# Block-end silu on other engines and a section later, transposes of the identity at the start, later stores of the split output weights

## The chip, the core and the metric

The kernel runs on one core of a Trainium2 chip. The metric is the device time of one execution in microseconds. The core's engines are TensorE (PE in the profile, its weight loads PEld), VectorE (DVE), ScalarE (ACT), GpSimd (POOL) and SyncE (SP), which here issues every DMA. Each engine works through its own queue in order; semaphores tie the queues together.

## The reference

One sequence of 2048 tokens with 576 features. The input is normalised and goes through two branches, whose product is added to the input:

```python
x = A_x
xn = _layernorm(x)
s = mha(xn, A_wqkv, A_wo)                    # 32 heads of 18, softmax, output projection
g = silu((gelu(xn @ B_w_gate) * (xn @ B_w_up)) @ B_w_down)   # 576 -> 4608 -> 576, tanh gelu
return x + s * g
```

All inputs and the output are float32.

## The kernel before

**Precision.** Matmul operands are kept as two parts, a rounded `hi` and the remainder `lo`, and most products are summed as hi·hi + lo·hi + hi·lo. `split` makes the parts on GpSimd (one `tensor_scalar`, one `tensor_tensor`), `split_av` on ScalarE and VectorE.

**Blocks.** Tokens are cut into NB = 4 blocks of TB = 512, four tiles of 128 each (index `j`).

**Prologue (pools `pro` and `pps`).** For block 0, `load_x` and `norm` bring in and normalise four tiles `xx`. `transposes` (line 205) turns them on TensorE against the identity `ident`: 20 transposes into five PSUM tiles `pt`, four tiles `j` by five slices `k`, all slices of one `j` first. `split_t` then writes the transposed activations `xth`, `xtl`, `xtr` from PSUM, ScalarE first and VectorE behind it. `project` (line 252) computes one 128-row tile of queries and keys per call, nine per block in the order `ORDER`, with 14 matmuls of 128x512 into a PSUM tile `po`; ScalarE and VectorE evict it and SP stores both parts to `qk` in DRAM. `values_of` does the values and stores them in `vs`. In the last block, `split_wo(n)` follows the projections 0 to 4: it loads a fifth of the output weights, splits it on GpSimd into two tiles `wo` (tag `rawp`, five buffers, shared with earlier weights) and stores both to `wos` in DRAM, from where they are read much later. These stores follow the load and the split directly in the program.

TensorE's order is written out by hand (`manual_schedule`); the order on the other engines is a scheduler's, except where `keep_in_program_order` holds an instruction. The DMAs, too, leave SP's queue in this order, and an issue that waits holds up all issues behind it.

**Main part.** The feed-forward branch is the spine. `section` (line 398) computes one 128-wide slice of the gate and up products for one token block: 27 pairs of matmuls into PSUM tiles `pg` and `pu`. There are 36 sections per block and 144 in all. Attention work (`specials`) is spread between the pairs: score maxima (`max_mm`, PSUM tile `pm` with three buffers, reduced on VectorE into `mx`), and scores for the exponentials (`score_mm`, PSUM tile `pe`, exponential on ScalarE into `pT`). At the end of a section `activate` applies the tanh GELU with ScalarE and VectorE; after it come the values' matmuls (`values`, PSUM `acc`), the down projection (`downs`, `down`, line 381, PSUM `py`) and `finish`, where GpSimd splits the activated slice into `hh` and `hl` and, every second section, the down weights into `dh` and `dl`. GpSimd also splits the next section's gate and up weights (`wh`, `wl`), and runs ahead of TensorE with them as far as the buffers let it.

**Down projection and block end.** A round of two sections gives one down projection, in two halves of two token tiles each, one section apart. Each half makes four pieces of 128x288 and adds them on VectorE into `Y`, the block's sum (line 387). `Y` is allocated anew in the first section of a block, in one buffer. In the last round of blocks 0 to 2 the half is followed by the silu of its four pieces, by `gate` (line 356): ScalarE computes `th = tanh(y/2)`, VectorE `(th + 1) * y` in place (line 359), and SP stores each 128x576 tile to `ys`. The factor one half comes later. The last block's pieces go through `gate` in the epilogue.

**Output projection.** `tasks` places its steps in later sections: `load_wo` reads `wos`, `load_xy` brings a piece of `x` and of `ys` into tiles `xx` (one buffer) and `yy` (two), `project_o` multiplies and adds, `store_y` writes `out`.

**The loop that matters to the change** (line 725): for each of its 128 passes `section`, the K, V and q loads, `tasks`, `values`, `downs`, `tasks`, `finish`. A block's last round ends in `downs` of the first two sections of the next block; in the span these are the sections that begin at 770.65 and 787.99, 1414.97 and 1432.32, 2059.83 and 2077.18 us.

Of the kernel before, what the change touches and what calls it, by code (L numbers as in the profile page):

```python
# [8 lines left out]
F32 = mybir.dt.float32  # L9
# [8 lines left out]
P = 128  # L18
# [33 lines left out]
def f(ap):  # L52
    return ap.bitcast(F32)
# [13 lines left out]
def kernel(ctx: ExitStack, tc: tile.TileContext, x, wqkv, wo, w_gate, w_up, w_down, out):  # L67
# [22 lines left out]
    def split(hi, lo, raw):  # L90
        first = nc.gpsimd.tensor_scalar(hi, raw, 1.0, 1.0, op0=ALU.mult, op1=ALU.mult)  # L91
        nc.gpsimd.tensor_tensor(lo, raw, f(hi), op=ALU.subtract)  # L92
        return first
# [41 lines left out]
    with tc.tile_pool(name="pro", bufs=1) as pro, tc.tile_pool(name="pps", bufs=1, space=PSUM) as pps:  # L135
# [45 lines left out]
        def norm(xr, b, between=None):  # L181
# [20 lines left out]
                nc.scalar.activation(xr[j][:, D:D + HR], xr[j][:, R0:D], AF.Copy)  # L202
            return last

        def transposes(b, xr):
            xt = XT[b % 2]
            pts = [pps.tile([P, TB], F32, name="pt", bufs=KT + 1) for k in range(KT + 1)]
            for j in range(4):
                for k in range(KT + 1):
                    nc.tensor.transpose(pts[k][:, j * P:(j + 1) * P], xr[j][:, k * P:(k + 1) * P], ident)  # L210
            for k in range(KT + 1):
                split_t(pts[k], k, xt)
            return xt
# [9 lines left out]
        VN = [pro.tile([P, H // 2, DH + 1], F32, name=f"vn{i}") for i in range(8)]  # L223
        for v in VN:
            nc.vector.memset(v, 1.0)
        ORDER = (4, 5, 0, 1, 6, 7, 8, 2, 3)
        WQK, WV = {}, {}

# [23 lines left out]
        def project(b, t, xt):  # L252
            o = pps.tile([P, TB], F32, name="po", bufs=3)
            mm_terms(o, WQK[t], slice(0, P), xt, all_t)
            hi, lo = tmp2("t1"), tmp2("t2")
            nc.scalar.activation(hi, o, AF.Copy)
            nc.vector.tensor_tensor(lo, o, f(hi), op=ALU.subtract)
            for i, a in enumerate((hi, lo)):
                nc.sync.dma_start(qk[i, t * P:(t + 1) * P, b * TB:(b + 1) * TB], f(a))
# [9 lines left out]
        def split_wo(k):  # L269
            n = min(KO, D - k * KO)  # L270
            raw = raw_tile([KO, D])
            tc.keep_in_program_order(nc.sync.dma_start(raw[0:n], wo[k * KO:k * KO + n, :]))
            hi, lo = (pro.tile([KO, D], F32R, name=f"wo{i}", tag="rawp", bufs=5) for i in range(2))
            split(hi[0:n], lo[0:n], raw[0:n])
            for i, t in enumerate((hi, lo)):
                nc.sync.dma_start(wos[i, k * KO:k * KO + n, :], f(t)[0:n])

        NQT = 2 * D // P
        def after(what, before):
# [19 lines left out]
        for b in range(NB):  # L299
            for n, t in enumerate(ORDER):  # L300
                if n == (2 if b == 0 else 0) and b + 1 < NB:
                    xr = load_x(b + 1)
                if b == 0 and ahead_qk:
                    first = split_qk(*ahead_qk.pop(0))
                    if n < 3:
                        after(first, last)
                    if n + 4 < NQT:
                        ahead_qk.append(load_qk(ORDER[n + 4]))
                if b == 0 and n == 4:
                    raw_r, VR = load_rest(2 * D, D)  # L310
                    split_av(VR[0], VR[1], raw_r, tc.keep_in_program_order)
                if b == 0 and n in (5, 6):
                    raw_v.append(load_wv(n - 5))
                if b == 0 and n in (7, 8):
                    split_wv(n - 7, raw_v[n - 7])
                project(b, t, xt)
                if b == NB - 1 and n < NK:
                    split_wo(n)
                if n == 4 and b + 1 < NB:
                    norm(xr, b + 1)  # L320
            store_xt(b, xt)
            nxt = transposes(b + 1, xr) if b + 1 < NB else None
            if b == 1:
                XD = load_xd(0)
            if b == 2:
                ahead = load_gu(0, tc.keep_in_program_order)
                for k in range(NG):
                    split_gu(ahead, k)
            for j in range(4):
                for c in range(2):  # L330
                    values_of(b, j, c, xt)
            xt = nxt
# [2 lines left out]
    ps = ctx.enter_context(tc.tile_pool(name="ps", bufs=1, space=PSUM))  # L335


    FF = {"w": ahead, "xd": XD, "down": [], "n": 0}
    finals = []

    def gate_up(tag):
# [14 lines left out]
    def gate(o, th, yy):  # L356

        nc.scalar.activation(th, yy, AF.Tanh, scale=0.5)
        nc.vector.scalar_tensor_tensor(o, th, 1.0, yy, op0=ALU.add, op1=ALU.mult)  # L359
# [11 lines left out]
    def down(b, r, hs, wd, Y, js):  # L371
        for j in js:
            tt = slice(j * P, (j + 1) * P)
            for c in range(2):
                cc = slice(288 * c, 288 * c + 288)
                py = ps.tile([P, 288], F32, name="py", tag="s", bufs=2)
                n = 0
                for g in range(G):
                    hh, hl = hs[g]
                    for a, w in ((hh, wd[0]), (hh, wd[1]), (hl, wd[0])):  # L380
                        nc.tensor.matmul(py, a[:, tt], w[:, g, cc], start=(n == 0), stop=(n == 3 * G - 1))  # L381
                        n += 1
                yy = Y[:, j, cc]
                if r == 0:
                    nc.vector.tensor_copy(yy, py)
                else:
                    nc.vector.tensor_tensor(yy, py, yy, op=ALU.add)  # L387
                if b == NB - 1 and r == NR - 1:
                    finals.append((Y, j, c))
        if b < NB - 1 and r == NR - 1:  # L390
            for j in js:
                t = b * 4 + j
                for c in range(2):
                    yy = Y[:, j, 288 * c:288 * c + 288]
                    gate(yy, ffn.tile([P, 288], F32, name="th"), yy)
                nc.sync.dma_start(ys[t * P:(t + 1) * P, :], Y[:, j, :])

    def section(specials=(), tag="f", raw_d=None, early=None):

        n = FF["n"]  # L400
        FF["n"] += 1
        b, r = divmod(n // G, NR)
        g = n % G
        pairs, pg, pu = gate_up(tag)
        if g == 0:
            FF["hs"] = []
            if r == 0:
                FF["Y"] = ffn.tile([P, TB // P, D], F32, name="Y")
        keep = tc.keep_in_program_order if n == NU * NA + len(FIRST) + 1 else lambda i: i
        nxt = load_gu((n + 1) % (NR * G), keep) if n + 1 < NF else None  # L410
        if nxt:
            for k in range(NG - 1):
                split_gu(nxt, k)
        if g == G - 1:
            raw = FF["rawd"] = raw_d() if raw_d else raw_tile([P, G, D])
            nc.sync.dma_start(raw, w_down[r * G * P:(r + 1) * G * P, :].rearrange("(g p) n -> p g n", p=P))
            if early:
                FF["wd"] = early(raw)
        for p in spread(pairs, specials):
            p()  # L420
        if nxt:
            split_gu(nxt, NG - 1)
        FF["w"] = nxt
        if n + 1 < NF and (n + 1) % (NR * G) == 0:
            FF["xd"] = load_xd(b + 1)
        FF["act"] = activate(pg, pu)
# [103 lines left out]
    def tasks(n, part):  # L530
        for t in todo.pop((n, part), []):
            t()
# [26 lines left out]
    with tc.tile_pool(name="att", bufs=1, reuse_waits="tile") as att:  # L559
# [32 lines left out]
        def load_q(u):  # L592
            j, g = divmod(u, NQ)
            cols = slice(j * TB, (j + 1) * TB)
            for r in range(2):
                t = QS[u, r] = att.tile([P, TB], F32R, name=f"q{r}", bufs=3)
                for a in range(2):
                    q = f(t)[64 * a:64 * a + MROW, :]
                    h = QD * g + 2 * r + a
                    rows = slice(h * DH, (h + 1) * DH)  # L600
                    for n, i in enumerate((0, 0, 1)):
                        nc.sync.dma_start(q[n * DH:(n + 1) * DH, :], qk[i, rows, cols])
# [122 lines left out]
        for n in range(NU * NA):  # L725
            u, i = divmod(n, NA)
            s0 = n * SLOTS
            section([p for s in range(s0, s0 + SLOTS) for p in slot_pairs(s)])
            if n > 0:
                load_k(n - 1 + KB)  # L730
            load_v(n + 2)
            if i == 1 and u + 2 < NU:
                load_q(u + 2)
            tasks(n, 0)
            um, im = divmod(s0 + LEAD + SLOTS, NS)
            if im == 0 and um <= NU:
                max_neg(um - 1)
            for kt in range(i * SLOTS // 2, (i + 1) * SLOTS // 2):
                values(u, kt)
            if im == 0 and um <= NU:  # L740
                max_end(um - 1)
            tasks(n, 1)
            downs()
            tasks(n, 2)
            finish()
# [86 lines left out]
```

## Time and profile before

| | us |
|---|---|
| median of 3 runs | 2670.77 |
| lowest and highest run | 2667.56, 2672.83 |
| the profiled execution | 2674.07 |
| its span, first to last instruction | 2672.3 |
| prologue, to the first `pg` matmul | 199.79 |
| a regular section, mean of four | 17.42 |

The profile is one execution, taken by the hardware profiler. A row of the timeline shows the start, the duration, the engine, the line and the operation with the tiles that it writes and reads; in square brackets, the idle time of the engine before it and what ended that. A row of the waits shows who waited for whom, the total, how often, and the longest. A row of the windows gives the stretch, its length, and each engine's busy time and number of instructions in it. A row of the groups has the smallest, median and largest duration in ns.

### The profile page before, as it was taken

The numbers are of one execution on the slowest core, as the hardware profiler recorded it, in microseconds if no ns is written. First come the engines' busy times: TensorE is split into PE (matmuls) and PEld (weight loads), VectorE is DVE, ScalarE is ACT, GpSimd is POOL, SyncE is SP. The second block draws the span as 40 slices with busy tenths as digits, with TensorE's granted clock in tenths as the row PEclk, the third lists the DMA queues.
The fourth block names the chain that finished last, engine by engine and source line by source line (L and its number), as shares of the span: only waits on it lengthen the run. The fifth ranks groups of instructions, "written<-read, shape, count | busy, mean of one in ns | idle before, by whom it ended". The sixth has DMA issues, their size and how long they took to land.

```text
span 2672.3 us, 55506 instructions
## 1 busy us (share of the span) xinstructions
PE 2648.8 (99%) x21000; PEld 2025.0 (76%) x21000; DVE 2007.3 (75%) x3432; ACT 1440.9 (54%) x2553; POOL 1354.0 (51%) x1439
## 2 busy tenths in 40 slices
PE   8999999999999999999999999999999999999999
PEld 7887777777777777777777777777777777777777
DVE  5327888888888877788888877788888877888445
ACT  3222466555666555566556655555666554666532
POOL 2117544544465555544456555554445556444563
PEclk9999999999999999999999999999999999999999
DMA  8866433344354334543346335433345454433341
GB/s 254 264 229 155 114 96 96 94 103 105 103 141 122 97 103 117 142 105 102 98 106 161 100 99 141 123 103 99 100 106 119 126 140 126 115 101 92 77 111 56
DMA packets 389143, 323.64 MB, mean 121 GB/s; under 512 B 105544, under 2 KB 302664, under 8 KB 388876
## 3 DMA queue, kind: packets, MB, share of 16 engines
q1 hardware_dynamic: 388876, 320.08, 44.8%
q8 instruction: 167, 2.74, 0.4%
q14 instruction: 100, 0.82, 0.1%
HBM read 266.58 MB, written 52.85 MB: 120 GB/s over the span
## 4 chain that ended last, share of the span: by engine, by line
PE 96%; DVE 2%; DMA 0%; ACT 0%; issue 0%; POOL 0%; SPq 0%; DVEq 0%
PE pg L351 27%; PE acc L673 17%; PE py L381 17%; PE pe L639 10%; PE pm L612 9%; PE pu L351 7%; PE po L156 7%; PE po L511 2%; DVE mx L613 1%; PE pt L210 0%; DVE Y L387 0%; DVE t L365 0%; DVE Y L359 0%; PE pm L622 0%; DMA xx<-in_A_x_dram 0%
## 5 line engine op out<-in xcount | busy, mean ns | idle before, releaser
L640 ACT ACTIVATE pT<-pe 128x512 f32<-128x512 f32 x2048 | 1165.3, 600 | 767.4 <-PE pm L612 610.7
L613 DVE TENSOR_REDUCE mx<-pm 128x1 f32<-128x512 f32 x2048 | 1295.2, 686 | 49.8 <-PE pm L612 29.2
L351 PE MATMUL pg<-xd,wh 64*128 64x512 f32 x2592 | 948.6, 398 | 0.5 <-issue 0.5
L351 PE MATMUL pu<-xd,wh 64*128 64x512 f32 x2592 | 946.5, 397 | 0.0
L639 PE MATMUL pe<-q,KS 56*128 56x512 f32 x2048 | 818.1, 407 | 0.1
L612 PE MATMUL pm<-KS,q 54*128 54x512 f32 x2048 | 799.5, 394 | 3.5 <-DVE mx L613 1.9
L91 POOL TENSOR_SCALAR wh<-raw 128x384 fp32r<-128x384 f32 x432 | 222.2, 515 | 882.6 <-DMA raw<-in_B_w_up_dram 516.0
L351 PEld LDWEIGHTS pg<-xd,wh 64*128 64x128 f32 x2592 | 483.3, 187 | 58.0 <-issue 22.6
L351 PE MATMUL pg<-xd,wl 64*128 64x512 f32 x1296 | 507.6, 392 | 0.0
L351 PE MATMUL pu<-xd,wl 64*128 64x512 f32 x1296 | 507.1, 391 | 0.0
L351 PEld LDWEIGHTS pu<-xd,wh 64*128 64x128 f32 x2592 | 483.6, 187 | 9.3 <-DVE t L368 1.4
L673 PE MATMUL acc<-pT,VS 128*32 128x512 f32 x4096 | 466.0, 595 | 0.0
L92 POOL TENSOR_TENSOR wl<-raw,wh 128x384 fp32r<-128x384 f32 x432 | 437.8, 1014 | 34.5
L639 PEld LDWEIGHTS pe<-q,KS 56*128 56x128 f32 x2048 | 369.3, 184 | 82.8 <-ACT pT L640 23.4
L612 PEld LDWEIGHTS pm<-KS,q 54*128 54x128 f32 x2048 | 377.2, 184 | 38.0 <-DVE mx L613 6.4
L387 DVE TENSOR_TENSOR Y<-py,Y 128x288 f32<-128x288 f32 x544 | 248.2, 457 | 203.5 <-PE py L381 202.6
L381 PE MATMUL py<-dh,hh 128*128 128x288 f32 x1152 | 357.6, 310 | 2.3 <-DVE Y L387 1.3
L381 PE MATMUL py<-dl,hh 128*128 128x288 f32 x1152 | 339.8, 295 | 0.0
L381 PE MATMUL py<-dh,hl 128*128 128x288 f32 x1152 | 338.5, 294 | 0.0
L673 PEld LDWEIGHTS acc<-pT,VS 128*32 128x32 f32 x4096 | 120.4, 109 | 275.8 <-issue 264.5
L381 PEld LDWEIGHTS py<-dh,hh 128*128 128x128 f32 x1152 | 216.0, 187 | 81.1 <-issue 41.1
L351 PEld LDWEIGHTS pg<-xd,wl 64*128 64x128 f32 x1296 | 242.1, 187 | 20.0
(110 smaller groups left out, 2811.6 us busy)
## 6 DMA issues: line engine op xcount, KB each, us to landing
KS<-qk SPq DMA_DIRECT2D x1536, 36.0 KB
raw<-in_B_w_gate_dram SPq DMA_DIRECT2D x144, 288.0 KB
raw<-in_B_w_up_dram SPq DMA_DIRECT2D x144, 288.0 KB
raw<-in_B_w_down_dram SPq DMA_DIRECT2D x68, 576.0 KB
VS<-vs SPq DMA_DIRECT2D x128, 152.0 KB
qk<-t SPq DMA_DIRECT2D x72, 256.0 KB
q<-qk SPq DMA_DIRECT2D x384, 36.0 KB
xd<-xhs SPq DMA_DIRECT2D x24, 384.0 KB
```

Of the source, the lines that this page charges most:

```text
L91: first = nc.gpsimd.tensor_scalar(hi, raw, 1.0, 1.0, op0=ALU.mult, op1=ALU.mult)
L92: nc.gpsimd.tensor_tensor(lo, raw, f(hi), op=ALU.subtract)
L156: nc.tensor.matmul(o, st, m, start=(i == 0), stop=(i == len(TERMS) - 1))
L351: nc.tensor.matmul(o, w[1 + wp][k][rr, c, :], xd[xp][k][rr, c, :], start=(i == 0), stop=(i == len(terms) - 1))
L381: nc.tensor.matmul(py, a[:, tt], w[:, g, cc], start=(n == 0), stop=(n == 3 * G - 1))
L387: nc.vector.tensor_tensor(yy, py, yy, op=ALU.add)
L511: nc.tensor.matmul(po[:, 0:288], o[x][0:n, k, :], OW[w][0:n, k, :], start=(m == 0), stop=(m == len(terms) - 1))
L612: nc.tensor.matmul(pm, QS[u, r][rr, t * P:(t + 1) * P], KS[(u * NA + c) % KB][r][rr, :], start=True, stop=True)
L613: nc.vector.tensor_reduce(MX[u][:, 2 * r + a, t, c:c + 1], pm, axis=AX.X, op=ALU.max)
L639: nc.tensor.matmul(pe, KS[(u * NA + c) % KB][r][rr, t * P:(t + 1) * P], QS[u, r][rr, :], start=True, stop=True)
L640: nc.scalar.activation(PT[u, kt][:, 2 * r + a, :], pe, AF.Exp, scale=SCALE)
L673: nc.tensor.matmul(ACC[u][32 * a:32 * a + 32, :], VS[(u * NA + c) % VB][:, v:v + 32], pt[:, a, :], start=(kt == 0), stop=(kt == NT - 1), s ...
```

## The change

- **Silu at block ends.** `down` no longer applies `gate` in blocks 0 to 2. It notes its pieces in a list, and a new function `gates`, called in every pass of the main loop between the loads and `tasks`, works on what is noted: ScalarE computes the tanh into a tile `th`, GpSimd adds one and multiplies by `Y` in two operations, and SP stores each 128x288 piece to `ys`. So each half is handled one section later than before. Three of the four tiles `th` take the buffers of `yy` and `xx`, which are not in use then.
- **One `Y`.** `Y` is allocated once, ahead of all blocks.
- **Identity transposes.** `warm(64)` issues 64 transposes of `ident` by itself into an unread `po` tile, ahead of the first transposes of block 0.
- **Stores of `wos`.** `split_wo` returns its tiles; `store_wo` stores them after the projection two later, held in program order.

```diff
+        def warm(n):
+
+            o = pps.tile([P, TB], F32, name="po", bufs=3)
+            for i in range(n):
+                nc.tensor.transpose(o[:, 0:P], ident, ident)
+
         def transposes(b, xr):
...
             for j in range(4):
+                if b == 0 and j == 0:
+                    warm(64)
                 for k in range(KT + 1):
...
             split(hi[0:n], lo[0:n], raw[0:n])
+            return k, n, hi, lo
+
+        def store_wo(k, n, hi, lo):
             for i, t in enumerate((hi, lo)):
-                nc.sync.dma_start(wos[i, k * KO:k * KO + n, :], f(t)[0:n])
+                tc.keep_in_program_order(nc.sync.dma_start(wos[i, k * KO:k * KO + n, :], f(t)[0:n]))
...
                 project(b, t, xt)
+                if b == NB - 1 and 2 <= n < NK + 2:
+                    store_wo(*parts.pop(0))
                 if b == NB - 1 and n < NK:
-                    split_wo(n)
+                    parts.append(split_wo(n))
...
-    FF = {"w": ahead, "xd": XD, "down": [], "n": 0}
+    FF = {"w": ahead, "xd": XD, "down": [], "gates": [], "n": 0,
+          "Y": ffn.tile([P, TB // P, D], F32, name="Y")}
...
         if b < NB - 1 and r == NR - 1:
-            for j in js:
-                t = b * 4 + j
-                for c in range(2):
-                    yy = Y[:, j, 288 * c:288 * c + 288]
-                    gate(yy, ffn.tile([P, 288], F32, name="th"), yy)
-                nc.sync.dma_start(ys[t * P:(t + 1) * P, :], Y[:, j, :])
+            FF["gates"] += [(b, j, c, Y) for j in js for c in range(2)]
+
+    def gates():
+
+        for k, (b, j, c, Y) in enumerate(FF["gates"]):
+            rows, cc = slice(b * TB + j * P, b * TB + (j + 1) * P), slice(288 * c, 288 * c + 288)
+            if k < 3:
+                th = op.tile([P, 288], F32, name="th", tag=("yy", "yy", "xx")[k], bufs=(2, 2, 1)[k])
+            else:
+                th = ffn.tile([P, 288], F32, name="th")
+            tc.keep_in_program_order(nc.scalar.activation(th, Y[:, j, cc], AF.Tanh, scale=0.5))
+            nc.gpsimd.tensor_scalar(th, th, 1.0, 1.0, op0=ALU.add, op1=ALU.mult)
+            nc.gpsimd.tensor_tensor(th, th, Y[:, j, cc], op=ALU.mult)
+            nc.sync.dma_start(ys[rows, cc], th)
+        FF["gates"] = []
...
         if g == 0:
             FF["hs"] = []
-            if r == 0:
-                FF["Y"] = ffn.tile([P, TB // P, D], F32, name="Y")
...
             load_v(n + 2)
             if i == 1 and u + 2 < NU:
                 load_q(u + 2)
+            gates()
             tasks(n, 0)
```

More of the change, by code (lines that the diff above doesn't have):

```diff
@@ L225 @@
             nc.vector.memset(v, 1.0)
+        parts = []
         ORDER = (4, 5, 0, 1, 6, 7, 8, 2, 3)
```

## The prediction

> **What bounds the kernel now.** I read the busy times first, then what TensorE (PE) waited for, then the length of like stretches, and last the timeline where these are longer than they should be.
>
> ```profile
> PE 2648.8 (99%) x21000; PEld 2025.0 (76%) x21000; DVE 2007.3 (75%) x3432; ACT 1440.9 (54%) x2553; POOL 1354.0 (51%) x1439
> ```
>
> PE is busy for 2648.8 of the 2672.3 us of the span; no other engine is above 76%. Time can be won where PE stands still, or where it keeps running with its matmuls further apart. The waits of PE alone list the first kind:
>
> ```profile
> PE pt L210 <- DVE xx L200: 10.9, 1, 10.9
> PE pm L612 <- DVE mx L613: 1.9, 4, 1.1
> PE pm L612 <- DMA q<-qk: 1.7, 2, 1.3
> ```
>
> The columns are total, number and longest. The start (10.9 us) and two later waits are all that matters. The second kind shows only in lengths. I cut the span at the first `pg` matmul of a section, so that each stretch below holds whole sections: four regular ones, then twice the four that follow a change of token block, then three with no block end and the three at the third block end.
>
> ```profile
> core 0 of [0], span 2672.3 us
> core 0: us, PE busy (x) PEld busy (x) DVE busy (x) ACT busy (x) POOL busy (x), PEclk, DMA share, GB/s
> 700.98:770.65 69.67, 69.67 (x572) 51.62 (x571) 57.09 (x96) 41.66 (x73) 37.16 (x39) 1.00 0.53 126
> 770.65:842.01 71.36, 71.11 (x571) 52.96 (x570) 60.66 (x104) 44.91 (x81) 40.02 (x42) 1.00 0.49 131
> 1414.97:1486.89 71.92, 71.57 (x572) 52.53 (x572) 61.16 (x104) 44.73 (x81) 41.18 (x43) 1.00 0.48 129
> 1990.15:2042.26 52.11, 52.11 (x427) 38.82 (x427) 42.27 (x70) 31.43 (x55) 29.73 (x31) 1.00 0.45 118
> 2059.83:2114.08 54.25, 53.96 (x428) 39.92 (x427) 46.21 (x78) 34.31 (x63) 37.68 (x36) 1.00 0.53 146
> ```
>
> The same PE work (571 or 572 matmuls; 427 or 428) takes 71.36 - 69.67 = 1.69, 71.92 - 69.67 = 2.25 and 54.25 - 52.11 = 2.14 us longer at the three block ends: 6.1 us. VectorE (DVE) and ScalarE (ACT) have eight instructions more there: the eight silu pieces.
>
> **Part 1, the silu.** The second half at one block end, in the timeline, and the group rows of its two operations:
>
> ```profile
> 1451.96 0.96 DVE L359 SCALAR_TENSOR_TENSOR Y<-th,Y 128x288 f32<-128x288 f32 x1
> 1452.84 0.68 DVE L613 TENSOR_REDUCE mx<-pm 128x1 f32<-128x512 f32 x1
> 1453.58 0.50 PE L612 MATMUL pm<-KS,q 54*128 54x512 f32 x1 [0.26 <-DVE mx L613]
> 1449.07 0.45 ACT L358 ACTIVATE th<-Y 128x288 f32<-128x288 f32 x1 [2.81 <-DVE Y L387]
> L358 ACT ACTIVATE th<-Y x24: 445/447/448, 786.2 to 2097.7; 128x288 f32<-128x288 f32 x24
> L359 DVE SCALAR_TENSOR_TENSOR Y<-th,Y x24: 448/696/1292, 786.9 to 2098.2; 128x288 f32<-128x288 f32 x24
> ```
>
> DVE takes its queue in order, and the silu products stand ahead of the reductions that free the score maxima's three PSUM buffers. The reduction of 1452.84 starts only behind the product of 1451.96, and PE waits for it at 1453.58. The change takes all 24 products off DVE (24 x 0.696 = 16.7 us of it); the additions into `Y` stay, and regular sections have those too. So I expect the excess of 6.1 us to go, and take 6.0. Upper bound 6.1.
>
> What it costs elsewhere. On ACT the four tanh of a half move from between the additions to the end of the next section, behind its GELU, where ACT stood idle 2.81 us (row of 1449.07). Four at 0.447 are 1.8 us and fit: nothing. Without that cover they would stand ahead of the exponentials, 1.8 us six times. On GpSimd (POOL) two operations per piece are new. Where they go, and who wants the work behind them:
>
> ```profile
> 802.17 0.51 POOL L91 TENSOR_SCALAR wh<-raw 128x384 fp32r<-128x384 f32 x1
> 802.76 1.02 POOL L92 TENSOR_TENSOR wl<-raw,wh 128x384 fp32r<-128x384 f32 x1
> 805.58 0.62 POOL L91 TENSOR_SCALAR hh<-t 128x512 fp32r<-128x512 f32 x1 [1.80 <-PE py L381]
> ...
> 809.06 2.75 POOL L92 TENSOR_TENSOR dl<-raw,dh 128x1152 fp32r<-128x1152 f32 x1
> 821.05 0.40 PE L381 MATMUL py<-dh,hh 128*128 128x288 f32 x1
> 824.46 0.49 PE L351 MATMUL pg<-xd,wh 64*128 64x512 f32 x1
> ```
>
> By elements a piece costs 0.51 x 288/384 + 1.02 x 288/384 = 1.15 us, a half 4.6 us (an estimate from these rows). The instruction order of the changed kernel puts the first half between `wl` (ends 803.78) and `hh` (805.58): 1.8 us of it fill an idle gap, and `hh`, `hl`, `dh` and `dl` come 2.8 us later. `dl` then ends at 814.6; PE asks for it at 821.05. The weight slices of 802.17 and behind are for the section that starts at 824.46, some 20 us on. The second half stands ahead of an `hh` that is wanted a section later still. So nothing again, with 6.4 us of slack. The stores of `ys` become 24 of half the size. They wait for GpSimd in SP's queue, ahead of two K loads, a V load, q loads and the next gate, up and down weights; the SP queue waited for the old stores at the same place, and these weights have those 20 us. Lower bound for this part: half of it, 3.0, should the added queueing of GpSimd reach the reductions in a way I don't see.
>
> **Part 2, the stores of the split output weights.** They stood in SP's queue right behind their load, so that SP waited for GpSimd's split, and later stores and loads with it:
>
> ```profile
> SPq L276 <- POOL wo L91: 8.4, 4, 4.1
> 187.97 0.41 ACT L266 ACTIVATE vn<-po 128x288 f32<-128x288 f32 x1 [1.01 <-PE po L156]
> 193.25 0.66 SPq L110 DMA_DIRECT2D raw<-in_B_w_gate_dram  x1
> 199.72 4.69 DMA vs<-vn
> 200.57 6.23 SPq L580 DMA_DIRECT2D KS<-qk  x12
> 206.85 3.95 SPq L602 DMA_DIRECT2D q<-qk  x11
> 209.35 0.46 PE L612 MATMUL pm<-KS,q 54*128 54x512 f32 x1 [1.34 <-DMA q<-qk]
> ```
>
> The first gate weights are issued at 193.25, though the value tile ahead of them was ready at 188.4: 4.9 us late. Their transfers are then still under way when the K loads begin: the last value store takes 4.69 us to land, and 12 K loads take 6.23 us where 11 q loads take 3.95 (0.36 each; 12 would take 4.3). The 1.9 us between are SP waiting for earlier transfers, and the q loads behind are what PE waits for (1.7 us in two waits). With the stores two projections later the split is done when their turn comes, the queue is level by 188, and the weights go up to 4.9 us earlier. Were all 1.9 us to go, the 1.7 us would go; were the memory itself the limit, nothing. The longest wait for a reduction (1.1 us, second row of PE's waits) comes ten microseconds later, and its chain leads back to that same landing by way of GpSimd's clearing of tiles. Bounds 0 and 1.7 + 1.1 = 2.8; I take 1.5, nearer the two q waits. The ten stores themselves cost nothing: the last is issued earlier than now.
>
> **Part 3, the idle transposes.**
>
> ```profile
> 1.01 0.29 POOL masks.py:199 TENSOR_SCALAR_AFFINE_SELECT ident<-ident 128x128 f32<-128x128 f32 x1
> 10.19 2.05 DVE L200 TENSOR_SCALAR xx<-xx,st 128x576 f32<-128x576 f32 x4
> 10.91 4.09 PE L210 MATMUL pt<-ident,xx 128*128 128x128 f32 x20 [10.91 <-DVE xx L200]
> 14.14 0.87 PE L210 MATMUL pt<-ident,xx 128*128 128x128 f32 x5
> ...
> 14.60 1.09 ACT L164 ACTIVATE xth<-pt 128x512 fp32r<-128x512 f32 x2 [1.87 <-PE pt L210]
> 45.37 2.34 PE L210 MATMUL pt<-ident,xx 128*128 128x128 f32 x20
> ```
>
> The first fifteen transposes come (14.14 - 10.91) / 15 = 0.215 us apart; the next block's take 2.34 / 20 = 0.117. So PE runs at about half pace for its first 3.4 us or so. In the change it starts at about 1.4, when the identity is there: 16 slow ones (3.4 us) and 48 fast ones (5.6 us) end at 10.4, ahead of 10.91. The real ones then run fast; the sixteenth, which the first split waits for, starts at 10.91 + 15 x 0.117 = 12.7 (its tile is normalised by 12.24) and not at 14.14: 1.5 us. All later work of PE up to 199.7 follows without a gap, so this carries on. If the slow stretch lasts twice as long, 32 + 32 transposes end at 1.4 + 6.9 + 3.7 = 12.0, and the gain is 0.4. If it never ends, 64 x 0.215 = 13.8 us: the real ones start at 15.2, slow, and lose 4.2 us. I take 1.3, near the case that the rows show.
>
> The Trainium skill ("TensorE: Matmul & The Clock Gate", Part 1) has the array's clock halved until a free-running window of some 3.4 us has been busy, so that a slow stretch lasts 3.4 to 6.8 us as the phase falls. By that rule this term is 0.4 to 1.5 us and the sum 7.9 to 9.0. The trace agrees on length and ratio; the phase of a run it doesn't show.
>
> **Sum.** 6.0 + 1.5 + 1.3 = 8.8 us. The profiled execution took 2674.07 (span 2672.3 and 1.8 around it), so 2665.3 in its terms. It lies 3.3 us above the median of the runs (2670.77); in theirs: 2662.0.
>
> **Rivals.**
> - *The block ends stay as long.* The reductions would be late anyway, by the additions and the GELU on DVE. For it: the first half of the first block end costs less than the rest. Against: the regular stretches have the same additions and none of the excess. Gain 2.8: 2668.0.
> - *The stores give nothing*, the memory being the limit. For it: the 4.69 us of one store. Against: SP waits 8.4 us for splits. Gain 7.3: 2663.5.
> - *The idle transposes stay slow*, and hold up the first block: 8.8 - 1.3 - 4.2 = 3.3: 2667.5. Against: the pace that doubles within 3.5 us in the rows above.
> - *GpSimd becomes the bound (slower).* The new operations read 288-wide pieces of a wider tile, which no GpSimd row has. `dl` may come 821.05 - 811.8 = 9.2 us later and 1.8 us are a gap, so PE waits from 11.0 us per half, 2.4 times my price. At four times (18.4 us) it waits 7.4 us at each of three first halves: 2662.0 + 22 = 2684. Against: the rows' prices per element (1.02/384, 2.75/1152) are alike, 2.4 to 2.7 ns.
>
> **How the numbers follow.** Forecast 0.63, stores worth nothing 0.10, block ends unchanged 0.12, slow transposes 0.08, slower 0.07. The likeliest gives 2662.0. Its own range: gains of 3.0 + 0 + 0.4 to 6.1 + 2.8 + 1.5, that is 3.4 to 10.4, and 1.5 us for the runs' scatter (2667.56 to 2672.83): 2659 to 2669. The range 2657.5 to 2669 holds all but the slower case and a little scatter. 0.2%, about what a measurement can tell, is 5.3 us: the first two cases are faster (0.73, 0.01 less for scatter), the next two the same, the last slower with 0.01 more.
>
> **What would show it.** Right: stretches of 52.1 and 69.7 us at the block ends; no `mx` wait there; no q wait of 1.3 us near 207; the first split near 13.0 in place of 14.60; eight POOL operations of 0.4 and 0.8 us per half. Wrong: PE waits on `dl` or `hh` at block ends, `pm` waits on q loads as long as now, or real transposes that begin after 11 us.

## The result and the profile after

| | before | after |
|---|---|---|
| median, us (8 runs each) | 2670.73 | 2661.33 |
| lowest and highest | 2667.56, 2672.83 | 2660.66, 2663.88 |
| the profiled execution | 2674.07 | 2661.96 |

The ratio is 0.9968 with a 95% interval of 0.9957 to 0.9979: 8.5 us faster by the ratio, between 5.6 and 11.5, and 9.4 by the medians. The forecast was 2662.0, 8.8 faster. One execution among all series, of p2_stores below, took 4664.64 us at a granted clock of 0.56 and is left out of that kernel's ratio.

The busy times of the changed kernel, and what TensorE waits for in it (total, number, longest):

```profile
PE 2648.3 (100%) x21064; PEld 2039.8 (77%) x21064; DVE 1991.7 (75%) x3408; ACT 1437.1 (54%) x2553; POOL 1381.0 (52%) x1487
```
```profile
PE po L209 <- POOL ident masks.py:199: 1.4, 1, 1.4
PE py L396 <- DVE Y L402: 1.0, 5, 0.2
PE pm L634 <- DVE mx L635: 1.0, 1, 1.0
PE pm L634 <- issue: 0.7, 1, 0.7
PE pm L634 <- DMA q<-qk: 0.6, 1, 0.6
```

PE's busy time is what it was, since the 64 idle transposes count as busy; the start no longer counts as idle. Of four waits for a reduction (`mx`) one is left, at 216.74 us and so at no block end. The two waits near 207 us (0.7 and 0.6, one of them without a releaser in the records) replace the 1.3 and 0.3 of before.

The stretches that the prediction compared, in the windows of the changed kernel: four regular sections, the first two block ends, three regular sections, the third block end.

```profile
697.96:767.45 69.49, 69.49 (x572) 52.48 (x571) 56.89 (x96) 41.59 (x73) 37.84 (x40) 1.00 0.53 127
767.45:837.01 69.56, 69.56 (x572) 52.21 (x571) 56.92 (x96) 44.28 (x81) 47.98 (x57) 1.00 0.50 136
1409.01:1478.51 69.50, 69.50 (x571) 52.10 (x571) 56.92 (x96) 44.27 (x81) 47.45 (x57) 1.00 0.50 135
1981.22:2033.25 52.03, 52.03 (x427) 39.26 (x426) 42.14 (x70) 31.39 (x55) 29.73 (x31) 1.00 0.46 118
2050.77:2102.82 52.05, 52.05 (x428) 39.26 (x428) 42.11 (x70) 34.07 (x63) 40.28 (x46) 1.00 0.48 131
```

A block end is now as long as a regular stretch (69.56 and 69.50 against 69.49; 52.05 against 52.03). DVE's count is that of a regular stretch, POOL has 15 to 17 instructions and 10 us more, and PE doesn't notice. The three block ends became 1.80 + 2.42 + 2.20 = 6.4 us shorter. Some 0.4 us of this is the pace of the whole execution, since the regular stretches are shorter too: each set against the regular stretch of its own execution, the excess fell from 6.1 us to 0.1.

GpSimd's timeline through both halves of the first block end, and the first TensorE row that wants the down weights of the first half:

```profile
799.66 0.84 POOL L417 TENSOR_SCALAR th<-th 128x288 f32<-128x288 f32 x2
800.45 1.58 POOL L418 TENSOR_TENSOR th<-th,Y 128x288 f32<-128x288 f32 x2
...
804.31 0.63 POOL L91 TENSOR_SCALAR hh<-t 128x512 fp32r<-128x512 f32 x1
...
807.53 2.68 POOL L92 TENSOR_TENSOR dl<-raw,dh 128x1152 fp32r<-128x1152 f32 x1
...
816.04 0.40 PE L396 MATMUL py<-dh,hh 128*128 128x288 f32 x1
...
819.39 0.83 POOL L417 TENSOR_SCALAR th<-th 128x288 f32<-128x288 f32 x2
...
824.76 1.29 POOL L92 TENSOR_TENSOR hl<-t,hh 128x512 fp32r<-128x512 f32 x1
```

The four pieces of a half take 804.31 - 799.66 = 4.65 us (forecast 4.6). `dl` ends at 810.21, 5.8 us before TensorE's row (forecast 6.4).

The start, in the timelines of TensorE and of ScalarE:

```profile
1.36 9.79 PE L209 MATMUL po<-ident 128*128 128x128 f32 x64 [1.36 <-POOL ident masks.py:199]
11.02 2.40 PE L218 MATMUL pt<-ident,xx 128*128 128x128 f32 x20
```

```profile
13.02 1.58 ACT L164 ACTIVATE xth<-pt 128x512 fp32r<-128x512 f32 x3
```

The first split starts at 13.02, where it was 14.60. And SP's queue around the first section, which begins at 197.87, with what is left of SP's waits for the split output weights:

```profile
187.05 0.66 SPq L110 DMA_DIRECT2D raw<-in_B_w_gate_dram  x1
...
194.47 0.60 SPq L110 DMA_DIRECT2D raw<-in_B_w_up_dram  x1
195.96 2.16 SPq L276 DMA_DIRECT2D vs<-vn  x2
198.21 0.31 SPq L624 DMA_DIRECT2D q<-qk  x1
198.61 5.49 SPq L602 DMA_DIRECT2D KS<-qk  x12
SPq L288 <- POOL wo L92: 1.5, 3, 0.7
```

SP waits 1.5 us for these splits, where it was 13.7 (8.4 for one step of the split and 5.3 for the other). The first gate weights go out 6.2 us earlier than before (1.9 of it is the earlier start). But the K loads stand behind the last two value stores, and those wait for ScalarE's eviction of the last values (`vn`). The K loads start 0.74 us after the first gate matmul, as before (200.57 against 199.79).

### The profile page after: what moved, and what is told of

It is laid out like the page before. It is cut to its first block, busy times and chain, and to the rows that moved or that the text cites. A ratio compares the mean times of both kernels' runs of the same rounds, so it can differ in the third digit from the quotient of the medians.

```text
span 2660.2 us, 55706 instructions
## 1 busy us (share of the span) xinstructions
PE 2648.3 (100%) x21064; PEld 2039.8 (77%) x21064; DVE 1991.7 (75%) x3408; ACT 1437.1 (54%) x2553; POOL 1381.0 (52%) x1487
## 4 chain that ended last, share of the span: by engine, by line
PE 97%; DVE 2%; DMA 0%; ACT 0%; issue 0%; SPq 0%; POOL 0%; DVEq 0%; POOLq 0%
PE pg L366 28%; PE py L396 17%; PE acc L695 17%; PE pe L661 10%; PE pm L634 8%; PE po L156 7%; PE pu L366 6%; PE po L533 2%; DVE mx L635 0%; PE po L209 0%; PE pt L218 0%; DVE t L380 0%; DVE Y L402 0%; PE pm L644 0%; DMA pT<-in_B_w_down_dram 0%
```

## The experiments

Three series, each with the kernel before timed between the others on the same chip: 2670.68, 2671.68 and 2672.97 us. Stretches are taken from each run's own profile, from the first gate matmul of one section to that of another. "Start" runs from the first real transpose to the first split; "K" is the time in which SP issues the first 12 K loads.

| series | kernel | sections 9 to 36 | 36 to 40 | 72 to 76 | 108 to 111 | 0 to 3 | start | K |
|---|---|---|---|---|---|---|---|---|
| first | before | 470.75 | 71.36 | 71.92 | 54.25 | 28.35 | 3.69 | 6.23 |
| first | after | 469.79 | 69.56 | 69.50 | 52.05 | 27.90 | 2.00 | 5.49 |
| 1 | p1_silu | 469.82 | 69.47 | 69.57 | 52.02 | 26.93 | 3.69 | 4.67 |
| 1 | p2_stores | 469.90 | 71.85 | 71.47 | 54.10 | 28.02 | 3.69 | 4.51 |
| 1 | p3_warm | 469.79 | 71.92 | 71.10 | 54.73 | 27.25 | 1.95 | 5.08 |
| 1 | a0_after | 469.73 | 69.53 | 69.50 | 52.00 | 26.95 | 1.94 | 4.51 |
| 2 | b0_before | 470.35 | 71.47 | 71.65 | 54.09 | 27.15 | 3.46 | 4.88 |
| 2 | s1_dve_later | 470.32 | 72.93 | 75.40 | 55.37 | 28.63 | 3.68 | 5.78 |
| 2 | s2_pool_now | 470.19 | 69.73 | 73.10 | 52.03 | 26.64 | 3.58 | 4.54 |
| 2 | g1_pool_x4 | 470.19 | 93.60 | 94.96 | 62.97 | 26.76 | 1.95 | 4.50 |
| 3 | n1_no_stores | 470.28 | 69.65 | 69.50 | 52.07 | 28.22 | 1.94 | 5.86 |
| 3 | p2b_stores | 470.29 | 71.36 | 71.40 | 54.22 | 26.88 | 3.53 | 4.53 |
| 3 | w40 | 470.29 | 69.51 | 69.64 | 52.01 | 26.58 | 2.01 | 4.50 |
| 3 | w16 | 470.29 | 69.57 | 69.59 | 52.03 | 27.43 | 3.71 | 4.52 |

### Each part alone, and the whole again

The silu part alone is the changed kernel with

```diff
-                    warm(64)
+                    pass
...
-                tc.keep_in_program_order(nc.sync.dma_start(wos[i, k * KO:k * KO + n, :], f(t)[0:n]))
+                nc.sync.dma_start(wos[i, k * KO:k * KO + n, :], f(t)[0:n])
...
-                if b == NB - 1 and 2 <= n < NK + 2:
-                    store_wo(*parts.pop(0))
...
-                    parts.append(split_wo(n))
+                    store_wo(*split_wo(n))
```

and the other two are the kernel before with the change's own lines for the stores, or for `warm(64)`.

p1_silu:

> Only the silu's part of the change (tanh on ScalarE and two operations on GpSimd, a section later, one Y); no idle transposes, old order of the output weights' stores. Theory A (the parts are independent, and this one takes away the excess at the three block ends and nothing else): 6.0 us faster than before, 5 to 7.5; the four-section stretches at the block ends as long as regular ones (within 0.1 us), start and q waits as before (first split at 14.6 us, two q waits of 1.6 us together). Rival B (the regular sections, which were 0.03 us shorter each in the profile after, are shortened by this part too, some 3.5 us over the span): 9 to 10 us faster, and its regular sections 0.03 us shorter than those of before in its profile as well.

p2_stores:

> Only the later stores of the split output weights. Theory A (the q loads stay behind twelve K loads that still wait for the gate and up weights): 0.4 us faster than before, between 0 and 0.8, which this measurement can hardly tell from nothing; the two q waits of TensorE go from 1.66 us to about 1.3 in its profile. Rival B (the whole of the wait goes, and what kept it in the profile after was the earlier start of that kernel): 1.5 to 2 us faster, q waits under 0.3 us.

p3_warm:

> Only the 64 idle transposes. Theory A (they take up TensorE's slow stretch before the first tile is there, and all later work follows): 1.6 us faster than before, 0.4 to 1.8 by where the slow stretch ends; twenty real transposes 0.109 us apart from the first on, the first split near 13.0 us in place of 14.6. Rival B (the time comes back as a wait further on, since the transfers are no earlier): within 0.3 us of before, with longer waits of TensorE at the q loads near 206 us.

a0_after:

> The whole change again, beside its parts on one chip. Theory A (additive): 6.0 + 0.4 + 1.6 = 8.0 us faster than before, and within 1.5 us of the sum of the three parts as measured. Rival B (the parts help one another): more than 1.5 us better than their sum.

| | median | ratio to before | gain of the medians, us |
|---|---|---|---|
| p1_silu | 2664.12 | 0.9977 [0.9968, 0.9985] | 6.6 |
| p2_stores | 2667.99 | 0.9990 [0.9981, 0.9999] | 2.7 |
| p3_warm | 2668.42 | 0.9994 [0.9985, 1.0003] | 2.3 |
| a0_after | 2660.96 | 0.9964 [0.9952, 0.9977] | 9.7 |

By the ratios the gains are 6.1, 2.7, 1.6 and 9.6 us. The three parts add up to 11.6 us by the medians and 10.4 by the ratios, against 9.7 and 9.6 for the whole. Each part's interval reaches some 2.4 us to either side, so the parts are additive as far as these times can tell, and theory A's 8.0 is 1.6 short.

The table of stretches tells the parts apart more sharply than the times do. The block ends are short in the two kernels with the silu part and long in the two without; the start is short in the two with the idle transposes and long in the others. The windows of p2_stores at the block ends look like those of before:

```profile
769.03:840.88 71.85, 71.14 (x571) 52.46 (x571) 61.20 (x104) 44.65 (x81) 40.48 (x42) 1.00 0.49 130
1412.87:1484.34 71.47, 70.85 (x571) 52.46 (x570) 60.81 (x104) 44.78 (x81) 41.34 (x43) 1.00 0.47 130
2056.30:2110.40 54.10, 53.83 (x427) 39.91 (x426) 45.97 (x78) 34.26 (x63) 37.32 (x36) 1.00 0.53 145
```

The regular stretch of sections 9 to 36 is 469.7 to 469.9 in all four, with or without the silu. So the 1 us by which it is longer in the first profile of before is not the products' doing. One thing was not as expected: TensorE waited 0.4 us for the q loads in p1_silu, with the old stores, where 1.6 was expected, and 1.5 in p2_stores, with the later ones.

### Before once more

Unchanged, to see how much of its first profile is that one execution.

> The kernel before, unchanged, profiled a second time. Theory (the first profiled execution of it, 2674.07 us, ran slower as a whole and not through its block ends alone): the regular stretches come out as in the four later profiles, 469.8 us for sections 9 to 36 and 572.1 for 40 to 72 in place of 470.75 and 572.95, the block ends stay at 71.4 to 71.9 and 54.2, and the profiled execution takes 2670 to 2672 us. Rival (the silu on VectorE lengthens the regular sections too): 470.7 and 572.9 again. The ratio is 1.000 by both, within 0.1%.

Ratio 0.9998 [0.9989, 1.0007]; the profiled execution took 2670.17. The block ends stay, 71.47, 71.65 and 54.09. The regular stretch is 470.35: neither number expected, but all other kernels of series 2 and 3 have 470.2 to 470.35 as well, and those of series 1, on another chip, 469.8. The regular pace goes with the chip and the execution. The start took 3.46 us and the 12 K loads 4.88 in place of 6.23; so the profile that the prediction was made from had a slow draw of the K loads.

### The silu a section later, but on VectorE

Only the silu part, with

```diff
-            nc.gpsimd.tensor_scalar(th, th, 1.0, 1.0, op0=ALU.add, op1=ALU.mult)
-            nc.gpsimd.tensor_tensor(th, th, Y[:, j, cc], op=ALU.mult)
+            nc.vector.scalar_tensor_tensor(th, th, 1.0, Y[:, j, cc], op0=ALU.add, op1=ALU.mult)
```

> Only the silu part, and with the product left on VectorE (one operation a piece, as before) but a section later, behind that section's reductions for the scores' maxima; stores and start as before. Theory (what cost 6 us was the products' place ahead of the reductions): the four stretches at the block ends come down almost as far as in p1_silu, 69.5 to 70.0 and 52.1 to 52.5, the time is 2664 to 2666. Rival (VectorE simply has four products too many there, 2.8 us of work per half, wherever they stand): the stretches stay at 71.4 to 71.9 and 54.2, the time is 2669 to 2671.

2678.18 us, ratio 1.0023 [1.0012, 1.0034]: slower than before by 6.5, which neither theory said. VectorE's timeline at the second half, and the row of TensorE that waits for it:

```profile
819.34 1.23 DVE L415 SCALAR_TENSOR_TENSOR th<-th,Y 128x288 f32<-128x288 f32 x1
820.49 0.67 DVE L381 SCALAR_TENSOR_TENSOR t<-t,pu 128x512 f32<-128x512 f32 x1
821.09 2.66 DVE L415 SCALAR_TENSOR_TENSOR th<-th,Y 128x288 f32<-128x288 f32 x3
823.67 0.81 DVE L398 COPY Y<-py 128x288 f32<-128x288 f32 x2
```
```profile
824.17 0.40 PE L394 MATMUL py<-dh,hh 128*128 128x288 f32 x1 [2.39 <-DVE Y L398]
```

A section later the products no longer stand ahead of the reductions but ahead of the evictions of `py`, which has two PSUM buffers. PE waits 2.39 us for the first of them, and the wait comes back at the other two block ends (2.44 and 2.37). So it is not the place alone: on VectorE the products stand ahead of something that TensorE wants, at both places tried.

The second block end is the longest, 75.40 us. Behind its wait of 2.44 us, which ends at 1470.62, the granted clock is 0.50 from 1471.9 to 1475.3; behind the waits of 2.39 and 2.37 it stays at 1.00.

The four take 3.9 us in the rows above; alone they would take 1.8 (four at 0.445). The group row:

```profile
L415 DVE SCALAR_TENSOR_TENSOR th<-th,Y x24: 443/745/1514, 801.3 to 2115.7; 128x288 f32<-128x288 f32 x24
```

By the Trainium skill ("SBUF — State Buffer", section "Who interferes with whom") a VectorE instruction with two SBUF inputs contends with a GpSimd instruction that reads SBUF. The trace agrees: of the 24 products, the seven with no GpSimd instruction beside them take 445 or 446 ns, and the fourteen with 0.35 us or more of GpSimd's splits beside them take 621 to 1514.

### On ScalarE and GpSimd, but at once

Only the silu part, with `gates()` moved behind `downs()` of its own section.

```diff
-            gates()
             tasks(n, 0)
...
             downs()
+            gates()
             tasks(n, 2)
```

> Only the silu part, on ScalarE and GpSimd as in the change, but at once behind the half's additions and not a section later; stores and start as before. Theory (no product on VectorE ahead of the reductions, so no wait): block ends 69.5 to 69.9 and 52.0 to 52.4, the time 2664 to 2666. Rival (the tanh then stand ahead of the next section's exponentials on ScalarE, as the prediction priced the case without cover, 1.8 us six times): block ends 3 us longer than in p1_silu, 72 to 73 and 54 to 56, the time 2672 to 2675.

2666.24 us, ratio 0.9980 [0.9971, 0.9990]: 5.4 faster, most of what the silu part brings. Two block ends are as short as with the change (69.73, 52.03), so it is the engine that matters, and the tanh cost ScalarE nothing at their old place either. The second block end has a new wait, in TensorE's timeline:

```profile
1459.21 0.40 PE L394 MATMUL py<-dh,hh 128*128 128x288 f32 x1
1461.36 0.40 PE L394 MATMUL py<-dl,hh 128*128 128x288 f32 x1 [1.75 <-POOL dl L92]
...
1462.16 0.44 PE L394 MATMUL py<-dh,hl 128*128 128x288 f32 x1
...
1464.80 0.44 PE L394 MATMUL py<-dl,hh 128*128 128x288 f32 x1
...
1465.65 0.29 PE L394 MATMUL py<-dh,hh 128*128 128x288 f32 x1
```

There GpSimd's eight operations came late enough to hold `dl` up. In p1_silu, a section later, TensorE has no such wait. The wait is 1.75 us long but the stretch is 3.6 us longer; the rows show where the rest is. After the wait the matmuls stand 0.24 us apart until 1465.04, then 0.13, and the windows have a granted clock of 0.57 in that piece:

```profile
1461.30:1465.00 3.70, 3.64 (x16) 3.64 (x17) 0.92 (x2) 0.00 (x0) 1.49 (x3) 0.57 0.59 142
```

### Four times GpSimd's work

The whole change, with nine operations more per piece:

```diff
+            for _ in range(9):
+                nc.gpsimd.tensor_scalar(th, th, 1.0, 1.0, op0=ALU.mult, op1=ALU.mult)
             nc.gpsimd.tensor_tensor(th, th, Y[:, j, cc], op=ALU.mult)
```

> The whole change with nine operations more on GpSimd per piece (each a multiplication by 1.0 in place, 128x288), which bring a half from 4.6 us to some 18.4. The prediction's slower rival, whose point was 11.0 us a half: TensorE waits some 7.4 us for the down weights at each of three first halves, +22 us, 2683 us. Bounds: if an added operation takes 0.3 us in place of 0.38, a half takes 15.4 us and the wait is 4.4 us each, +13; if the second half delays work as well, up to six waits, +44. Rival (there is more cover than the prediction counted, through the lead of the weight slices): under 5 us, 2661 to 2666.

2737.08 us, ratio 1.0243 [1.0228, 1.0258]: with the whole change at 0.9966 (it had 0.9968 and 0.9964) that is 74 us, above all bounds. TensorE's timeline, and ScalarE's, at the first block end:

```profile
818.91 0.61 PE L396 MATMUL py<-dh,hh 128*128 128x288 f32 x1 [3.85 <-POOL dh L91]
822.72 0.61 PE L396 MATMUL py<-dl,hh 128*128 128x288 f32 x1 [3.20 <-POOL dl L92]
...
856.89 0.61 PE L396 MATMUL py<-dh,hh 128*128 128x288 f32 x1 [13.63 <-DVE Y L400]
```
```profile
852.45 0.60 ACT L379 ACTIVATE t<-pg 128x512 f32<-128x512 f32 x1 [14.35 <-POOL hl L92]
```

The first half is as priced: 18.8 us on GpSimd, and 3.85 + 3.20 = 7.05 us of waiting for the down weights, where the rival had 7.4. The second half costs twice that, by a way that the prediction did not have. GpSimd's `hl` reads the activated slice in tile `t` (`t1` in the program), which has one buffer; ScalarE's first step of the next section's GELU writes that tile. It waits 14.35 us for `hl`, VectorE's GELU waits for it, the evictions of `py` stand behind that, and PE waits 13.63. In the changed kernel `hl` ends at 824.76 + 1.29 = 826.05, and this step of ScalarE follows at 830.20:

```profile
830.20 0.59 ACT L379 ACTIVATE t<-pg 128x512 f32<-128x512 f32 x1
```

That is 4.15 us of room, so the rival's point is some 4.65 + 4.15 = 8.8 us a half (an estimate from these rows), and not 11.0. The measured wait is longer than this room explains (18.8 - 8.8 = 10.0 us): GpSimd's second half also began 4.0 us behind its section's first matmul (831.27 against 827.27), where in the changed kernel the two come together (819.39 and 819.46).

The waits of the three block ends add up to 60 us. The other 14 are matmuls at the slower pace behind them: the window of sections 36 to 40 has a mean clock of 0.89.

### The stores again

n1_no_stores is the whole change with the old stores (the first diff of the experiments without its `warm(64)` line); p2b_stores repeats p2_stores.

> The whole change without its store part: the split output weights are stored right behind their split, as before. Theory A (the later stores give something, as their timing alone said, 2.7 us with an interval of 0.3 to 5.1): 1.5 to 2.7 us slower than the whole change, 2662.5 to 2664 where the whole change took 2661.0. Theory B (the profiles' stretch of the first three sections, 26.6 to 28.6 us with the old stores and 26.8 to 28.0 with the new ones, is the whole of it): no difference beyond 0.5 us, 2661 to 2661.5, ratio to before 0.9964 to 0.9966.

p2b_stores:

> The store part alone, a second time. Theory A: 1.5 to 2.7 us faster than before, ratio 0.9990 to 0.9994. Theory B: within 0.5 us of before, ratio 0.9998 to 1.0002. In the profile, either way: the output weights' stores wait no longer, the first gate weights are issued near 187 us in place of 193.

n1_no_stores took 2663.21, ratio 0.9964 [0.9951, 0.9976], the same as the whole change had in series 1 (0.9964): theory B. p2b_stores took 2670.58, ratio 0.9992 [0.9983, 1.0001], 2.4 us faster: theory A. On the same chip the whole change with 40 idle transposes (below) is 0.4 us faster than n1_no_stores. The times leave anything from 0 to 2.7 us.

The profiles show one thing clearly. SP's rows in n1_no_stores and in a0_after:

```profile
198.24 5.86 SPq L600 DMA_DIRECT2D KS<-qk  x12
```
```profile
197.76 4.51 SPq L602 DMA_DIRECT2D KS<-qk  x12
```

With the later stores the 12 K loads take 4.50 to 4.53 us in six of seven profiles (5.49 in one), with the old ones 4.54 to 6.23: means of 4.65 and 5.29. The first three sections take 27.22 us on average with the later stores and 27.60 without, each spread over 1.5 to 2 us. So what the profiles show is 0.4 us, within their scatter.

What the K loads wait for tells more. In two of the seven profiles with the old stores they waited for the gate and up weights, 1.6 us in before and 1.1 in s1_dve_later; in none of the seven with the later stores. That is 2.7 us in seven profiles, or 0.4 each: as far as these profiles show, it is what the later stores take away. In the changed kernel's first profile and in n1_no_stores they waited instead for the last value store, 1.0 and 1.2 us. And TensorE's waits for the q loads go from 0.4 to 1.7 us with the old stores and from 0.3 to 1.5 with the later ones; p2_stores has 1.5 although its K loads took only 4.51 us.

### Fewer idle transposes

`warm(64)` becomes `warm(40)` and `warm(16)`.

> The whole change with 40 idle transposes in place of 64. They end at 7.4 us (16 slow at 0.213, 24 at 0.109) to 8.9 us (30 slow), 1 to 3.6 us ahead of the first normalised tile. Theory (the pace stays up over a pause that is shorter than the slow stretch): the real ones run at 0.109 from their first and start 0.14 us behind their tile, the first split is 1.95 to 2.1 us behind them, the time 2660 to 2662. Rival (any pause puts the array back to the slow pace): 0.213 again, the first split 3.5 us behind the first transpose, the time 2662 to 2663.5.

w16:

> The whole change with 16 idle transposes. They end at 4.8 us, all of them slow, with a pause of 5 to 6 us before the first normalised tile. Theory (the fast pace has to be earned by work just before, and a pause longer than the slow stretch loses it): the real ones start at 0.213 and stay there for 3 to 4 us, the first split comes 3.5 us behind the first transpose, the time is 1.5 us above the whole change, 2662.5. Rival (one busy stretch is enough for good): 0.109 from the first real one, 2661.

w40 took 2662.77, ratio 0.9962 [0.9948, 0.9975], w16 2664.21, ratio 0.9967 [0.9955, 0.9979]. TensorE's start in w40 and in w16:

```profile
1.36 7.16 PE L209 MATMUL po<-ident 128*128 128x128 f32 x40 [1.36 <-POOL ident masks.py:199]
11.38 2.40 PE L218 MATMUL pt<-ident,xx 128*128 128x128 f32 x20 [2.87 <-DVE xx L200]
```
```profile
1.36 3.67 PE L209 MATMUL po<-ident 128*128 128x128 f32 x16 [1.36 <-POOL ident masks.py:199]
10.92 4.43 PE L218 MATMUL pt<-ident,xx 128*128 128x128 f32 x20 [5.90 <-DVE xx L200]
```

After a pause of 2.87 us the 20 real transposes take 2.40 us, after one of 5.90 they take 4.43, as without any idle ones. Both theories of a pace that has to be earned just before hold; 16 are as good as none. The start of the two differs by 1.7 us, the medians by 1.4.

## Why the prediction came out

**Part 1, right.** Forecast 6.0 us with bounds of 3.0 and 6.1. The excess went entirely: 0.07, 0.01 and 0.02 us are left of 6.08, so 6.0 us. The 6.4 by which the block ends are shorter contains the pace of the two executions; the part alone gave 6.6 by the medians and 6.1 by the ratio. The step "DVE takes its queue in order, and the silu products stand ahead of the reductions" is borne out by s2_pool_now, where taking them off VectorE at the same place brings 5.4. s1_dve_later adds that the later place on the same engine is worse than the old one. The stretches came out at 69.5 and 52.05 in place of 69.7 and 52.1 because the whole execution ran faster.

**Its costs, right at this size.** ScalarE nothing, as the first and third block ends of s2_pool_now show even without the move: the prediction's "without that cover they would stand ahead of the exponentials" did not happen. GpSimd's 4.6 us a half measured 4.65, and nobody waits. The statement on the second half ("wanted a section later still", so only the 6.4 us of the first half counted) overlooked the single buffer of `t`. At this size it changes nothing; from some 8.8 us a half it would have.

**Part 2, the term that was mis-sized.** Forecast 1.5 us; the profiles show some 0.4, the runs nothing between n1_no_stores and the whole change, and 2.4 to 2.7 with the part alone, so its size stays open between 0 and 2.7. Three steps failed. "The weights go up to 4.9 us earlier" was true of the first (6.2 us), but the K loads start some 0.75 us behind the first gate matmul in either order, since the last value stores ahead of them wait for the eviction of the last values. The 1.9 us between 6.23 and 4.3 were rightly read as SP waiting for earlier transfers, but taken for what the queue always costs; other profiles with the old stores have 4.5 to 5.9. And "were all 1.9 us to go, the 1.7 us would go" does not hold: with K loads of 4.50 to 4.53 us TensorE still waits 0.3 to 1.5 us for the q loads. The wait of 1.1 us for a reduction, in the upper bound, stays at 1.0 in every profile.

**Part 3, right, and slightly more.** Forecast 1.3 us, 1.5 without allowance; the first split came at 13.02 in place of 14.60, 1.58 us, and the start is 1.94 to 2.01 us with the idle transposes against 3.46 to 3.69 without. The runs of p3_warm say 2.3 by the medians and 1.6 by the ratio, with an interval that takes in 0. The idle ones had 25 slow ones and not 16, and ended at 11.15 and not 10.4; other profiles had 16, 21, 23 and 28. The mark "real transposes that begin after 11 us" was set wrongly: they began at 11.02, but in that execution their tile was ready at 10.96. In a0_after they began 0.45 us behind their tile, against 0.15 without idle ones, so 64 were some three more than that execution had time for (0.30 us at 0.109).

**The sum.** The prediction's three terms come out at 6.0 + 1.6 + 0.4 = 8.0 us in the profiles. A fourth, which it does not have, is at the end of the program: from VectorE's last instruction to the end of the span it takes 2.59 us and not 3.18. The stretch from the last section's first gate matmul to the end shows the same, 28.77 to 28.83 us in the eight kernels with the silu on GpSimd and 29.36 to 29.41 in the five without any change to the silu. So this 0.6 us comes with the silu part; why is open. The total is then 8.6 us, against 8.5 by the ratio [5.6, 11.5], 9.4 by the medians and 8.8 forecast. That the forecast is so near is in part luck: 1.1 us too much for the stores stand against 0.6 at the end and 0.3 at the start. Setting the sum against the profiled execution's own time and then taking off the 3.3 us by which it was above the median was needed: the two profiled executions differ by 12.1 us, and the regular stretches alone differ by about 3.

**The rivals.** Unchanged block ends and slow idle transposes fell. "The stores give nothing" (2663.5) can't be told from the forecast by the times. The slower one was right on its first coupling and missed a second, larger one and the slow pace behind the waits.

## What to carry to other kernels

An operation that delays a bottleneck from a strictly ordered queue is best moved to an engine with room; before moving it later on the same engine, list what TensorE waits for next in that queue. A wait of a DMA queue in one profile is one draw: take a second profile of the same kernel before pricing it, and look for the instruction that the transfers will still stand behind once the wait is gone. Slack on a helper engine ends at its nearest consumer, and a single buffer that it has to release is a consumer too.

## What the runs showed of the hardware

- **A wait can cost more than its length.** In s2_pool_now a wait of 1.75 us was followed by some 3.3 us of matmuls at half pace (0.24 us apart in place of 0.13), and the stretch is 3.6 us longer; in g1_pool_x4 some 14 of 74 us are of this kind. In s1_dve_later one of three like waits (2.44 us) was followed by 3.4 us at a granted clock of 0.50 and two (2.39 and 2.37) were not. Nor was the pause of 2.87 us in w40. Length alone doesn't decide it; what does, no run here shows. The Trainium skill ("TensorE: Matmul & The Clock Gate", section "HAM oscillation — how this bites in real kernels") gives as the rule no idle gaps of TensorE above some 3.4 us. The runs differ: a slow stretch followed waits of 1.75 and 2.44 us.
- **The slow stretch at the start varies.** With idle transposes it had 16 to 28 of 0.213 us, 3.4 to 6.0 us; in b0_before, with real ones alone, 3.0 us. The Trainium skill ("TensorE: Matmul & The Clock Gate", Part 1) has a free-running window of some 3.4 us; the spread agrees, and the 3.0 us lie a little below a whole window.
- **The same kernel's regular stretch** of 27 sections took 469.7 to 469.9 us in series 1 and 470.2 to 470.4 in series 2 and 3, on other chips: 0.1%, about 2.7 us of the whole.
